# A gated mix of linear attention and feed-forward on one core: the odd feature tiles of both first token blocks placed behind the keys, roundings placed ahead of the SiLU, and another order of work into the queries

## The chip, the cores and the metric

The kernel runs on 1 core of one Trainium2 chip. The metric is the time of one execution in device microseconds. The kernel before was timed three times: the median is 782.44 us, the lowest run 778.98 us, the highest 783.22 us. One further execution was profiled.

## The reference

The input x has 2048 tokens of 640 numbers. Two branches are computed from it and mixed by a gate per token:

```python
g = sigmoid((x * gate_w).sum(-1, keepdims=True))
# branch a: linear attention, 32 heads of 20, w_phi per head
pq, pk = q @ w_phi, k @ w_phi            # per head
phi_q = concat([softmax(pq), softmax(-pq)]);  phi_k likewise
o = (phi_q @ (phi_k.T @ v)) / (phi_q @ phi_k.T.sum(tokens) + 1e-6)
a = o @ wo
# branch b: feed-forward, 1728 features
b = silu(x @ w1) @ w2
out = g * a + (1 - g) * b
```

All inputs and the output are float32.

## The kernel before, in words

Tokens lie along the free dimension for most matmuls. A float32 operand goes to TensorE (PE) as two rounded parts, a high and a low one: ScalarE (ACT) rounds the high part by a copy (L117), and VectorE (DVE) or GpSimd (POOL) subtracts it from the source for the low part (L119). Each product is then three passes: high x high, high x low, low x high (`PASSES`). The weight's low part comes last.

The work goes through five stages.

1. **Keys and values.** 16 tiles of 128 tokens (`t`). For each, `kv_proj` (L497) projects keys and values into three PSUM banks `kvp0` to `kvp2`; DVE and ACT make the two softmaxes (`k_spikes`, exp, `k_sums`), and `kv_acc` (L467) and `kv_rest` (L478) add phi_k^T v of the tile two places back into the banks `kv0` to `kv4` and into the end of `kvp2`. `kv_rest` overwrites its place in each round, so VectorE has to have added the last round to `kra` (`kv_rest_sum`, L491) before PE may go on.
2. **Behind the keys** (`t = NT - 1`, all in one hand-written order). The first feed-forward products use `kvp0` and `kvp1` while the last key tile is finished.
3. **Feed-forward, layer 1.** The tokens are 4 blocks of 512; blocks 0 and 1 are treated together, and then 2 and 3. 12 of the 13 full feature tiles go in 6 pairs. Two token blocks x two feature tiles are computed with seven products in place of eight (`product`, numbers 1 to 7, L583, 6 or 9 matmuls each), from sums and differences of the weights (`w_sums`, POOL) and of the inputs (the tiles `xt1` to `xt4`). So there are 12 pairs, `n` = 0 to 11: `h_begin` does products 1 and 2, `h_rest` products 6, 7, 4, 5, 3. Between them stand hooks (`between`), lists of small pieces of work that `plan` fills: the weights of pair n+1 are rounded in four pieces (`w_parts`, a, c, b, d), those of pair n+2 are loaded (`w_load`), and tiles of the second two blocks are loaded (`x_raw`), summed (`t_sums`, L1040) and rounded (`n_parts`, `t_parts`). The tile 12 ("l", 128 features) and the rest ("r", 64 features) are plain products (`h_std`, L537). Each result is put through SiLU on ACT and stored in DRAM (`u_out`, `r_out`).
4. **Queries.** For 16 tiles of 128 tokens: projection (L455), two softmaxes, normalisation, transposes (L1139), product with the key sums (L1223), output projection (L1256). The first four tiles (8 to 11) are done between the plain products of blocks 2 and 3; the passage to the regular rhythm (`step`) is written out by hand.
5. **Feed-forward, layer 2** (L1477), with the mix at its end.

`inorder(...)` keeps PE, DVE, ACT and POOL in the order of the program from stage 3 on, and ACT, DVE and POOL (behind the keys PE too) in stage 1 and 2. So an instruction that waits holds all that is queued behind it on its engine. SyncE (SP) issues the DMAs; its order is chosen when the program is scheduled, and a DMA that waits for its buffer holds those behind it.

Buffers that matter: `raw`, 4 buffers for loaded inputs and early results; `w`, 9 buffers for weights and their parts; 8 PSUM banks.

Two lines show how PE and the other engines are tied in a pair before the change:

```python
todo[7] += [do(w_parts, n + 1, "a"), do(w_parts, n + 1, "c")]
todo[3] += [do(w_load, n + 2)]
```

Product 7 is followed by products 4, 5 and 3, and then by product 1 of the next pair, which reads piece a.

Of the kernel before, what the change touches and what calls it, by code (L numbers as in the profile page):

```python
# [16 lines left out]
P = 128  # L17
# [41 lines left out]
def mix_kernel(ctx: ExitStack, tc: tile.TileContext, xT, wqT, wkc, wkr, wv, bd, bdc, cst, wo, w1, w1r, w2, out):  # L59
# [211 lines left out]

    def w_parts(n, k, eng="dve"):
        e, s = WR[n]
        t = W.setdefault(n, {})[k] = two(f"ws{n}{k}")
        if k == "b":
            split(t[:, 0, : 3 * P], t[:, 1, : 3 * P], e[:, D : D + 3 * P], eng)
            split(t[:, 0, 3 * P :], t[:, 1, 3 * P :], s[:, : 2 * P], eng)
        else:
            parts(t, e[:, :D] if k == "a" else s[:, 2 * P : 6 * P] if k == "c" else s[:, 6 * P : 9 * P], eng)
# [265 lines left out]

    def u_out(f, b, src, early=False):
# [4 lines left out]
    def r_out(b, src, early=False):  # L551
# [3 lines left out]
        nc.scalar.activation(o, o, AF.Silu)  # L555
        nc.sync.dma_start(u_d[NF, :FR, b * 512 : (b + 1) * 512], o)
# [35 lines left out]
    def h_begin(n, between=None, banks=None):  # L592
        between = between or {}
        s, p = divmod(n, NQ)
        done = between.get(0, [])
        for part in done:
            part()
# [9 lines left out]
        for part in between.get(1, ()):  # L607
            part()
        p2 = banks.pop(0) if banks else bank(f"p{n}_2")
        product(n, 2, p2)  # L610
        add(p2, p2, first)
        u_out(2 * p, 2 * s, p2, banks is not None)
        for part in between.get(2, ()):
            part()

    def h_rest(n, between):
        s, p = divmod(n, NQ)
# [8 lines left out]
        def after(k):  # L626
            for part in between.get(k, ()):
                part()

        p6 = mm(6)  # L630
        if second is None:
# [3 lines left out]
        p7 = mm(7)  # L635
        r = fu.tile([P, 2, 512], F32, tag="u", name=f"r{n}", bufs=3)
        add(r[:, 0, :], p7, second)
        after(7)
        p4 = mm(4)
        add(p4, p4, r[:, 0, :])  # L640
        u_out(f1, b0, p4)
        after(4)
        p5 = mm(5)
        add(r[:, 1, :], p5, second)
# [3 lines left out]
        p3 = mm(3)  # L648
        add(p3, p3, r[:, 1, :])
# [9 lines left out]
    def kv_out():  # L659

        kvm = ta.tile([P, 2, 2 * D], F32, tag="ph", name="kvm", bufs=2)[: KF + 1, 0, :]
        kvl = ta.tile([P, 2, 2 * D], F32, tag="ph", name="kvl", bufs=2)[: KF + 1, 0, :]
        for k in range(len(kvt) + 1):
            n = 2 if k < len(kvt) else 1
            lo, hi = 2 * k * KF, min((2 * k + 2) * KF, 2 * D)
            w = (hi - lo) // n
            a, b = (ap[:, lo:hi].rearrange("p (g f) -> p g f", f=w) for ap in (kvl, kvm))
# [4 lines left out]
            else:  # L672
                kv_rest_sum(NT - 1)
                nc.vector.tensor_tensor(b, kra[:, :1, RW - w :], kra[:, 1:, RW - w :], op=ALU.add)
            mask = cstt[: KF + 1, None, :w].to_broadcast([KF + 1, n, w])
            nc.gpsimd.tensor_tensor(b, b, mask, op=ALU.mult)
        kvo.extend((kvl, kvm))
# [14 lines left out]
    def n_split(b, c, t, eng="dve"):  # L692
# [12 lines left out]
        12: [lambda: w_parts(1, "a", "pool")],  # L705
# [3 lines left out]
    with inorder(ACT, DVE, POOL):  # L709
# [36 lines left out]
        with inorder(PE):  # L746
# [10 lines left out]
            n_split(0, 4, slot("xn0_4"), "pool")  # L757
# [3 lines left out]
            for k in (1, 2):  # L761
# [3 lines left out]
            b11, b21, b12 = rx[0, 0, 2], rx[0, 2, 2], rx[1, 0, 2]  # L765
            b22 = [rx[1, c] for c in (2, 3)]

            def less(o, i, j):
                nc.vector.tensor_tensor(o, i, j, op=ALU.subtract)

            less(b11, b12, b11)
            k_sums(t, eks[t])
            for k in (1, 2):
                v_part(t, k, 1)
# [804 lines left out]
```

## Time and profile before

| what | value |
|---|---|
| median of three runs | 782.44 us |
| the profiled execution | 781.32 us |
| its span, first to last instruction | 779.5 us |
| mean granted TensorE clock | 0.980 |
| PE busy | 744.7 us (96%), 4115 matmuls |
| VectorE busy | 451.9 us (58%) |
| ScalarE busy | 296.2 us (38%) |
| GpSimd busy | 331.8 us (43%) |

The span is 1.8 us shorter than the execution's own time. PE is without work in 34.8 us of the span (779.5 less 744.7). Busy is the union of the instructions, so a matmul's last part, in which the next could already have started, counts as busy.

### The profile page before, as it was taken

The page shows a single profiled execution, that of the slowest core. Times are in us where ns is not written, and L with a number is a line of the kernel's source. Part 1 is how long each engine was busy: PE and PEld are TensorE (multiplying, and loading weights), DVE is VectorE, ACT ScalarE, POOL GpSimd, SP SyncE. Part 2 cuts the span into 40 slices and gives each one's busy share as a digit, 9 for nine tenths or more (in the row PEclk, how much of TensorE's full clock was granted, in tenths as well). Part 3 has the DMA queues.
Part 4 walks back from the last instruction along what each step waited for, and adds up shares of the span by engine and source line. Part 5 has one row for each costly group of instructions (what it writes and reads, how often), then busy time and mean ns, then how long its engine had stood idle before and what let it go on. Part 6 is the DMA issues. An engine that isn't in the chain of part 4 may idle for free.

```text
span 779.5 us, 10978 instructions
## 1 busy us (share of the span) xinstructions
PE 744.7 (96%) x4115; PEld 643.4 (83%) x4115; DVE 451.9 (58%) x755; ACT 296.2 (38%) x548; POOL 331.8 (43%) x236
## 2 busy tenths in 40 slices
PE   9999999997899869999997999999998999999997
PEld 7888888885688648888986999999997888888886
DVE  5667666698647767654675776676552452232413
ACT  5344444445443354444536435433341422121110
POOL 2479888755537544133554665554300030020300
PEclk9999999999899979999998999999999999999999
DMA  9221121001443476545202111121147656172501
GB/s 317 93 69 55 34 69 34 15 0 35 145 164 114 153 226 186 184 146 172 80 0 61 55 62 56 51 69 35 35 139 236 195 166 193 48 245 76 175 26 67
DMA packets 49951, 83.41 MB, mean 107 GB/s; under 512 B 5448, under 2 KB 18904, under 8 KB 49898
## 3 DMA queue, kind: packets, MB, share of 16 engines
q1 hardware_dynamic: 49610, 82.20, 33.7%
q8 instruction: 32, 0.52, 0.3%
q10 hardware_dynamic: 288, 0.51, 0.2%
q14 instruction: 21, 0.17, 0.1%
HBM read 57.42 MB, written 25.27 MB: 106 GB/s over the span
## 4 chain that ended last, share of the span: by engine, by line
PE 56%; DMA 3%; DVE 3%; ACT 2%; issue 2%; POOL 1%; SPq 0%; DVEq 0%; ACTq 0%; POOLq 0%
PE acc L1477 24%; PE p L583 10%; PE pa L1256 9%; PE pq L455 7%; PE pn L1223 3%; PE pT L1139 2%; DMA xr<-xT 1%; PE pwq L229 1%; DMA w2rr<-w 1%; DMA wr<-w 1%; DVE eq L446 0%; DMA u_d<-u 0%; ACT eq L899 0%; PE pf L537 0%; POOL wt L270 0%
## 5 line engine op out<-in xcount | busy, mean ns | idle before, releaser
L1477 PE MATMUL acc<-u,w 128*128 128x512 f32 x780 | 179.4, 392 | 2.8 <-DVE pac L1271 2.8
L1477 PEld LDWEIGHTS acc<-u,w 128*128 128x128 f32 x780 | 147.4, 189 | 33.9 <-DVE pac L1271 3.0
L497 PE MATMUL kvp<-wh,xa 128*128 128x500 f32 (+1 forms) x420 | 92.9, 357 | 0.0
L1484 POOL TENSOR_TENSOR o<-o,y 128x512 f32<-128x512 f32 x15 | 20.2, 1381 | 152.9 <-DVE o L1483 152.9
L497 PEld LDWEIGHTS kvp<-wh,xa 128*128 128x128 f32 x420 | 71.6, 188 | 10.0
L1256 PE MATMUL pa<-oT,wo 128*128 128x256 f32 x600 | 79.6, 287 | 0.0
L119 DVE TENSOR_TENSOR u<-ur,u 128x512 fp32r<-128x512 f32 x52 | 36.1, 701 | 73.5 <-ACT u L117 73.4
L1256 PEld LDWEIGHTS pa<-oT,wo 128*128 128x128 f32 x600 | 76.1, 193 | 0.8 <-ACT oT L1232 0.8
L117 ACT CAST u<-ur 128x512 fp32r<-128x512 f32 x52 | 32.2, 623 | 107.9 <-PE acc L1477 75.1
L913 POOL TENSOR_TENSOR ez<-eq,zbc 128x1280 f32<-128x1280 f32 x16 | 47.0, 2939 | 43.2 <-ACT eq L899 43.2
L270 POOL TENSOR_TENSOR wt<-wr 128x256 f32<-128x256 f32 (+1 forms) x36 | 24.5, 681 | 83.9 <-DMA wr<-w 66.3
L548 ACT ACTIVATE u<-p 128x512 f32<-128x512 f32 x46 | 27.5, 598 | 85.0 <-issue 58.9
L119 POOL TENSOR_TENSOR ph<-ek,ph 128x1280 fp32r<-128x1280 f32 x16 | 47.4, 2963 | 28.1 <-ACT ph L117 28.1
L949 POOL TENSOR_TENSOR eq<-eq,sm 128x1280 f32<-128x1280 f32 x16 | 37.9, 2368 | 34.9 <-DVE sm L943 31.5
L497 PE MATMUL kvp<-wl,xa 128*128 128x500 f32 (+1 forms) x210 | 47.5, 356 | 0.0
L525 POOL TENSOR_TENSOR ek<-ek,st 128x1280 f32<-128x1280 f32 x16 | 37.9, 2369 | 7.7 <-ACT v L316 3.6
L497 PEld LDWEIGHTS kvp<-wl,xa 128*128 128x128 f32 x210 | 36.3, 189 | 5.4
L316 ACT CAST v<-kvp 128x360 fp32r<-128x360 f32 (+2 forms) x45 | 13.5, 336 | 69.8 <-PE kvp L497 66.5
L1483 DVE TENSOR_TENSOR o<-acc,G 128x512 f32<-128x512 f32 x20 | 13.7, 692 | 41.4 <-PE acc L1477 33.4
L455 PE MATMUL pq<-wq,xb 128*128 128x320 f32 x240 | 37.2, 312 | 0.0
L455 PE MATMUL pq<-wq,xn 128*128 128x320 f32 x240 | 36.8, 310 | 0.1
L455 PEld LDWEIGHTS pq<-wq,xn 128*128 128x128 f32 x240 | 35.6, 188 | 1.1 <-issue 0.4
(431 smaller groups left out, 1448.9 us busy)
## 6 DMA issues: line engine op xcount, KB each, us to landing
u_d<-u SPq DMA_DIRECT2D x52, 256.0 KB, 2.5
ur<-u_d SPq DMA_DIRECT2D x52, 256.0 KB, 4.2
wr<-w SPq DMA_DIRECT2D x24, 320.0 KB, 4.6
y<-fb_d SPq DMA_DIRECT2D x20, 256.0 KB, 5.9
out<-o SPq DMA_DIRECT2D x20, 256.0 KB, 4.5
w2r<-w SPq DMA_DIRECT2D x13, 320.0 KB, 3.3
fb_d<-pac SPq DMA_DIRECT2D x16, 256.0 KB, 2.1
xra<-xT SPq DMA_DIRECT2D x14, 256.0 KB, 3.3
```

Of the source, the lines that this page charges most:

```text
L117: nc.scalar.copy(hi, src)
L119: eng.tensor_tensor(lo, src, hi.bitcast(F32), op=ALU.subtract)
L270: nc.gpsimd.tensor_tensor(o[k], x, y, op=op)
L455: nc.tensor.matmul(dst, xt[c][:, hx, :], w[:, c, hw, lo : lo + n], start=first, stop=(hx == 1 and c == NC - 1))
L497: nc.tensor.matmul(kv_cols(t, lo, hi), xt[c][:, hx, :], WKV[hw][:, c, lo:hi], start=(n == 0), stop=(n == 3 * NC - 1), skip_group_check=True,)
L525: nc.gpsimd.tensor_tensor(groups(e), groups(e), spread(st[:, 1, :]), op=ALU.mult)
L548: nc.scalar.activation(o, src, AF.Silu)
L583: nc.tensor.matmul(dst, W[n][w][:, hw, j * P : (j + 1) * P], x[:, hx, :], start=(i == 0), stop=(i == len(todo) - 1))
L913: nc.gpsimd.tensor_tensor(ez, Q[t]["e"], kvb["zbc"], op=ALU.mult)
L949: nc.gpsimd.tensor_tensor(groups(q["e"]), groups(q["e"]), spread(q["sm"][:, 2 * H : 4 * H]), op=ALU.mult)
L1256: nc.tensor.matmul(pa[:, a, :], kvb["wo"][:, c, hw, ds] if c < NG else WOR[:, ds], o[:, ho, c, :] if c < NG else o[:GW, 0, c, :], start=(k ...
L1477: nc.tensor.matmul(acc[m], lhs, rhs, start=(f == OF[0] and n == 0), stop=(f == OF[-1] and n == len(todo) - 1))
```

## The change

It does four things.

1. **Roundings are cut into two halves.** `steps` gives a pair of functions, one that issues the high parts (ACT), one that issues the low parts (DVE or POOL). A hook entry that is such a pair is now issued in two places: its high part before the add that ends the product, hence ahead of that product's SiLU on ACT, and its low part behind it.
2. **Behind the keys** the plain tiles of block 1 follow those of block 0 on PE, and the last key sums (`kv_acc(15)`, `kv_rest(15)`) stand between and behind them; before, block 1's plain tiles came after pair 0, and the last key sums inside pair 1. Only pair 0 is begun in this stage (before: pairs 0 and 1). The block differences and their roundings are cut in halves of 512 and dealt out differently to DVE and POOL. The masking of the key sums comes before `w_sums(1)`. Block 1's first two chunks are no longer loaded a second time, and pair 1's piece a is no longer rounded during key tile 12.
3. **In the pairs**, piece a of pair n+1 is rounded at product 2 instead of 7, piece c at 6 instead of 7; the weights of pair n+2 are loaded after product 2 instead of 3; the tiles of blocks 2 and 3 are loaded, summed and rounded earlier and in smaller portions.
4. **Into the queries**, three instead of four transposes of the first tile pair stand before the next projection; the plain rest of block 3 stands ahead of `n_mm`; the SiLU of the last three results, with its table, moves from the passage into `step(2)`, and the two rests of blocks 2 and 3 share one tile for it; the softmax of query tile 12 comes ahead of other work on DVE and ACT.

The number of matmuls is the same (3950 matmul instructions in both programs).

The diff, cut to its core:

```diff
+    def steps(*pairs, eng="dve"):
+        def high():
+            for hi, lo, src in pairs:
+                nc.scalar.copy(hi, src)
+        def low():
+            for hi, lo, src in pairs:
+                less(lo, src, hi.bitcast(F32), eng)
+        return high, low
...
+    def hooks(between):
+        def before(k):
+            for part in between.get(k, ()):
+                if isinstance(part, tuple):
+                    part[0]()
+        def after(k):
+            for part in between.get(k, ()):
+                (part[1] if isinstance(part, tuple) else part)()
+        return before, after
...
         p2 = banks.pop(0) if banks else bank(f"p{n}_2")
         product(n, 2, p2)
+        before(2)
         add(p2, p2, first)
         u_out(2 * p, 2 * s, p2, banks is not None)
-        for part in between.get(2, ()):
-            part()
+        after(2)
...
-            less(b11, b12, b11)
             k_sums(t, eks[t])
+            n_split(0, 4, slot("xn0_4"))
...
+            for c in (2, 3):
+                n_split(1, c, room(1, c + 2, 1))
             for k in (1, 2):
                 v_part(t, k, 1)
             kv_rest_sum(t - 2)
             h_std("l", kvp[0], n1, range(NC))
             u_out(NF - 1, 0, kvp[0], True)
+            phs[t] = k_split(t, eks[t])
+            for c in range(2):
+                n_split(1, c, room(0, c + 4, 1))
+            n_split(1, 4, slot("xn1_4"))
...
             h_std("r", kvp[1], n1, range(NC))
             r_out(0, kvp[1], True)
             kv_rest(t - 1, phs[t - 1], True)
             kv_acc(t - 1, phs[t - 1])
+            kv_rest_sum(t - 1)
+            h_std("l", kvp[0], n2, (2, 3, 0, 1, 4))
+            kv_acc(t, phs[t])
+            u_out(NF - 1, 1, kvp[0], True)
+            h_std("r", kvp[1], n2, (2, 3, 0, 1, 4))
+            kv_rest(t, phs[t], True)
...
-            h_begin(0, {1: [four]}, banks)
-            two_parts()
-            h_begin(1, {1: [key_sums, lambda: parts(xt[3], b12), lambda: parts(xt[4], b21, "pool")]}, banks)
-            w_sums(1)
-            kv_out()
+            h_begin(0, {1: [t_four, lambda: kv_sums(slice(1))], 2: [*x4, lambda: kv_sums(slice(1, None))]}, [kvp[0], kvp[1]])
+            kv_mask()
+            w_sums(1)
...
         if n + 1 < 2 * NQ:
             todo[0] += [do(w_sums, n + 1)]
-            todo[7] += [do(w_parts, n + 1, "a"), do(w_parts, n + 1, "c")]
-            todo[4] += [do(w_parts, n + 1, "b")]
-            todo[5] += [do(w_parts, n + 1, "d")]
+            todo[2] += [w_steps(n + 1, "a")]
         if n + 2 < 2 * NQ:
-            todo[3] += [do(w_load, n + 2)]
+            todo[2] += [do(w_load, n + 2)]
+        if n + 1 < 2 * NQ:
+            todo[6] += [w_steps(n + 1, "c")]
+            todo[4] += [w_steps(n + 1, "b")]
+            todo[5] += [w_steps(n + 1, "d")]
...
             if n == 5:
-                todo[2] += [do(x_raw, *bc) for bc in ((2, 4), (3, 4), (3, 2), (3, 3))]
-                todo[5] += [do(n_parts, 0, 4), do(n_parts, 1, 4)]
+                todo[1] += [n_steps(0, 4)]
+                todo[7] += [n_steps(1, 4)]
+            if n == 4:
+                todo[4] += [do(x_raw, *bc) for bc in ((2, 4), (3, 4), (3, 2), (3, 3))]
...
-        t_all(0, range(4, 6))
         on(0, q_mm)
+        t_all(0, range(3, 6))
+        pf = single("pr3")
+        h_std("r", pf, n2, range(NC))
         n_all(0)
+        q_sum(11)
+        q_norm_sum(11)
+        q_parts(11)
         for gp in range(3):
             n_hi(0, gp)
-        pf = single("pr3")
-        h_std("r", pf, n2, range(NC))
-        q_sum(11)
-        more(11)
+        on(0, q_max)
+        q_inv(11)
+        q_weights(11)
+        q_mul(11)
+        r_both(3, pf, ur)
+        on(0, q_spread)
         on(1, q_mm)
-        late_out(NF, 2, ur2, FR)
-        late_out(NF - 1, 3, uf3)
-        ur3 = r_sum(3, pf)
-        late_out(NF, 3, ur3, FR)
+        on(0, q_norm)
         for gp in range(3):
             n_lo(0, gp)
+        on(1, q_max)
```

Three places show the order of the instructions, as the built programs have it. The names: `xn` and `xs` are rounded inputs of blocks 0 and 1, `rx` their raw tiles, `ek15` the exponents of the last key tile, `st15` their sums, `v0` the values, `kra` the running sum of `kv_rest`.

VectorE behind the keys, before, from the first sum of the last key tile's exponents:

```order
L523 TENSOR_REDUCE st15_1721<-ek15_1702 128x64
L524 RECIPROCAL st15_1721<-st15_1721 128x64
L318 TENSOR_TENSOR v0_110<-kvp2_80,v0_110 128x4x60
L318 TENSOR_TENSOR v0_110<-kvp2_80,v0_110 128x40
L491 TENSOR_TENSOR kra_363<-kvp2_80,kra_363 121x228
L119 TENSOR_TENSOR xs1_1730<-rx1_2_803,xs1_1730 128x512
L119 TENSOR_TENSOR xs1_1730<-rx1_3_805,xs1_1730 128x512
```

The same place in the changed kernel:

```order
L555 TENSOR_REDUCE st15_1712<-ek15_1699 128x64
L556 RECIPROCAL st15_1712<-st15_1712 128x64
L119 TENSOR_TENSOR xn0_4_1716<-rx0_4_1634,xn0_4_1716 128x512
L119 TENSOR_TENSOR xs1_1711<-rx1_2_803,xs1_1711 128x512
L119 TENSOR_TENSOR xs1_1711<-rx1_3_805,xs1_1711 128x512
L350 TENSOR_TENSOR v0_110<-kvp2_80,v0_110 128x4x60
L350 TENSOR_TENSOR v0_110<-kvp2_80,v0_110 128x40
L523 TENSOR_TENSOR kra_363<-kvp2_80,kra_363 121x228
```

Three subtractions that read two tiles of SBUF (`xn0_4`, `xs1` twice) now stand ahead of the add to `kra`; `xn0_4` was on POOL before.

ScalarE in pair 4, before, from its copy of product 1 (`q4`) to the SiLU that follows product 4 (`u0_9`); `u0_8` is the SiLU of product 2, `xn2` are tiles of block 2:

```order
L606 COPY q4_2373<-p4_1_2366 128x512
L548 ACTIVATE u0_8_2386<-p4_2_2375 128x512
L117 CAST xn2_1_2389<-xr2_1_2354 128x512
L117 CAST xn2_3_2392<-xr2_3_2358 128x512
L117 CAST ws5a_2412<-wr5_2349 128x640
L117 CAST ws5c_2415<-wt5_2360 128x512
L548 ACTIVATE u0_9_2429<-p4_4_2418 128x512
```

The same place in the changed kernel:

```order
L656 COPY q4_2385<-p4_1_2378 128x512
L279 CAST xt2_1937<-xr3_3_2220 128x512
L279 CAST ws5a_2399<-wr5_2288 128x640
L279 CAST xt3_1938<-xr3_1_2216 128x512
L584 ACTIVATE u0_8_2403<-p4_2_2389 128x512
L279 CAST ws5c_2418<-wt5_2372 128x512
L279 CAST xt4_1939<-xr2_3_2222 128x512
L279 CAST xt1_1936<-xr2_1_2218 128x512
L279 CAST ws5b_2445<-wr5_2288 128x384
L279 CAST ws5b_2445<-wt5_2372 128x256
L584 ACTIVATE u0_9_2449<-p4_4_2435 128x512
```

Piece a of pair 5 (`ws5a`) has moved ahead of the SiLU of product 2, piece b ahead of that of product 4, and the tiles `xt1` to `xt4` of the second half of the chunks have come from pair 5 into pair 4.

ScalarE on the way into the queries, before, from the last rounding of the first attention outputs (`oT0`) to the first copies of the second tile pair's transposes (`fT1`); `eq12` is the exponential of query tile 12:

```order
L1235 ACTIVATE oT0_3714<-pn0_2_3725,stk_94 120x256
L906 ACTIVATE sm11_3604<-sm11_3604,g_92 128x64
L907 ACTIVATE sm11_3604<-sm11_3604 128x32
L1170 ACT_TABLE_LOAD
L1170 ACTIVATE u2_r_3500<-u2_r_3500 64x512
L1170 ACTIVATE u3_12_3636<-u3_12_3636 128x512
L1165 COPY u3_r_3793<-pr3_3734 64x512
L1170 ACTIVATE u3_r_3793<-u3_r_3793 64x512
L847 ACTIVATE wor_h_3802<-wor_3665,stk_94 120x640
L899 ACT_TABLE_LOAD
L899 ACTIVATE eq12_3713<-eq12_3713 128x1280
L1155 COPY fT1_0_3832<-pT1_0_3817 120x512
```

The same place in the changed kernel:

```order
L1293 ACTIVATE oT0_3727<-pn0_2_3738,stk_94 120x256
L1227 COPY u23_r_3502<-pr3_3716 64x512
L963 ACTIVATE eq12_3698<-eq12_3698 128x1280
L911 ACTIVATE wor_h_3806<-wor_3661,stk_94 120x640
L1216 COPY fT1_0_3828<-pT1_0_3813 120x512
```

The two table loads and the three SiLUs are gone from this place.

More of the change, by code (lines that the diff above doesn't have):

```diff
@@ L590, in mix_kernel, with h_begin @@
     QS = {}
-    def h_begin(n, between=None, banks=None):
-        between = between or {}
+    def hooks(between):
[7 more added lines that the diff above has]
+        return before, after
+    def h_begin(n, between, banks=None):
+        before, after = hooks(between)
         s, p = divmod(n, NQ)
-        done = between.get(0, [])
-        for part in done:
-            part()
+        before(0)
+        after(0)
         p1 = banks.pop(0) if banks else bank(f"p{n}_1")
@@ L624, in mm @@
             return dst
-        def after(k):
-            for part in between.get(k, ()):
-                part()
         p6 = mm(6)
+        before(6)
         if second is None:
@@ L639, in h_rest @@
         p4 = mm(4)
+        before(4)
         add(p4, p4, r[:, 0, :])
@@ L648, in h_rest @@
         p3 = mm(3)
+        before(3)
         add(p3, p3, r[:, 1, :])
@@ L1194, in mix_kernel @@
         q_sum(10)
-        for i in range(4):
+        for i in range(3):
             t_mm(0, i, bank)
@@ L1319, in step @@
         t_all(u, range(3))
+        if u == 1:
+            on(b, lambda t: [q_sub(t, side) for side in range(2)])
+            on(a, q_sum)
         on(a, q_norm_sum, q_small, q_mul)
```

215 lines of the change are left out of this document (114 added, 101 removed).

## The prediction

> **What bounds the kernel now.** I read the page's engine rows first, then the waits of PE, then a table of PE's busy time and clock by stage, and last the timeline around each large wait.
>
> ```profile
> span 779.5 us, 10978 instructions
> PE 744.7 (96%) x4115; PEld 643.4 (83%) x4115; DVE 451.9 (58%) x755; ACT 296.2 (38%) x548; POOL 331.8 (43%) x236
> L119 DVE TENSOR_TENSOR u<-ur,u 128x512 fp32r<-128x512 f32 x52 | 36.1, 701 | 73.5 <-ACT u L117 73.4
> L117 ACT CAST u<-ur 128x512 fp32r<-128x512 f32 x52 | 32.2, 623 | 107.9 <-PE acc L1477 75.1
> ```
>
> PE is the bound, and the change leaves its matmuls as they are. So the time can fall only by what PE loses in waits and in slow clock. The other two rows give the price of one rounding of 512 columns: 0.62 us on ScalarE, 0.70 us on VectorE. PE's waits, the longest in total:
>
> ```profile
> PE p L583 <- ACT xn L117: 7.2, 1, 7.2
> PE pT L1139 <- ACT fT L1155: 5.6, 2, 4.5
> PE kvp L478 <- DVE kra L491: 3.4, 1, 3.4
> PE acc L1477 <- DVE pac L1271: 2.8, 1, 2.8
> ```
>
> Only the wait at L1477 lies in layer 2, where nothing is changed. The stages that the change touches, cut at the plain tiles behind the keys, at pair 1's product 6, at block 2's first plain tile and at the output projection, then four stretches of slow clock and one undisturbed stretch for scale:
>
> ```profile
> 172.98:216.28 43.30, 34.66 (x144) 26.54 (x142) 31.99 (x43) 20.75 (x39) 23.50 (x18) 0.92 0.30 94
> 216.28:377.61 161.33, 150.55 (x694) 124.65 (x693) 101.93 (x157) 74.50 (x147) 70.18 (x74) 0.96 0.52 164
> 377.61:435.50 57.89, 51.41 (x325) 45.46 (x323) 37.88 (x64) 25.90 (x44) 29.31 (x23) 0.94 0.12 35
> 250.00:260.00 10.00, 10.00 (x46) 8.28 (x45) 6.58 (x10) 3.38 (x7) 4.37 (x3) 1.00 0.67 220
> 192.23:199.06 6.83, 6.07 (x14) 4.79 (x15) 3.38 (x6) 5.03 (x10) 2.65 (x2) 0.50 0.22 77
> 267.32:270.73 3.41, 3.41 (x10) 2.64 (x9) 2.29 (x3) 1.30 (x3) 3.24 (x3) 0.50 0.11 42
> 289.48:294.63 5.15, 5.15 (x12) 4.08 (x13) 3.44 (x5) 2.69 (x5) 1.46 (x2) 0.50 0.90 293
> 425.72:431.16 5.44, 5.44 (x26) 5.40 (x27) 3.78 (x8) 2.15 (x5) 2.32 (x1) 0.50 0.00 0
> ```
>
> The columns are the stretch, its length, then busy time of PE, weight load, VectorE, ScalarE, GpSimd, then the clock, the DMA share and GB/s. PE is idle 8.6 us behind the keys (43.30 less 34.66), 10.8 us in the pairs, 6.5 us on the way into the queries: 25.9 us. In the slow stretches it works at half speed for 6.07 + 3.41 + 5.15 + 5.44 us, which costs half of that, 3.0 + 1.7 + 2.6 + 2.7 = 10.0 us. In the undisturbed stretch a 512-column matmul starts every 0.217 us (10.00 over 46).
>
> **Behind the keys.** Rows of before, from the timeline:
>
> ```profile
> 173.21 1.27 ACT L759 ACTIVATE ek<-ek 128x1280 f32<-128x1280 f32 x1
> 175.58 1.47 DVE L523 TENSOR_REDUCE st<-ek 128x64 f32<-128x1280 f32 x1
> 176.84 0.73 PE L537 MATMUL kvp<-xn,w_l 128*128 128x512 f32 x2 [0.74 <-POOL xn L119]
> 177.08 0.55 DVE L524 RECIPROCAL st<-st 128x64 f32<-128x64 f32 x1
> 177.41 2.47 PE L537 MATMUL kvp<-xn,w_r 128*128 128x512 f32 x10
> 177.78 2.37 POOL L525 TENSOR_TENSOR ek<-ek,st 128x1280 f32<-128x1280 f32 x1 [0.99 <-ACT xs L117]
> 177.92 0.39 DVE L491 TENSOR_TENSOR kra<-kvp,kra 121x228 f32<-121x228 f32 x1
> 178.22 3.08 DVE L119 TENSOR_TENSOR xs<-rx,xs 128x512 fp32r<-128x512 f32 x2
> 181.52 2.95 POOL L119 TENSOR_TENSOR ph<-ek,ph 128x1280 fp32r<-128x1280 f32 x1 [1.37 <-ACT ph L117]
> ```
>
> Ten matmuls take 2.47 us: nine starts 0.217 apart and a last one of 0.52. So a stop costs 0.3 us more than the gap shown, since the last matmul's tail counts as busy; with a dozen stops over 0.3 us in the three stages that is about 4 us, of which I put 2.2 here, 1.1 in the pairs, 0.8 in the passage. PE now loses here 8.6 + 2.2 + 3.0 = 13.8 us.
>
> Two subtractions of 0.70 us each took 3.08 us at 178.22: the first was held until GpSimd's 2.37 us operation ended at 180.15. The add to kra, which reads PSUM, was not held. [...]
>
> The new order step by step, with these durations. The exponential no longer waits behind a cast, so the sum starts near 173.5, the reciprocal ends near 175.5; the low part of xn0_4 follows on VectorE and ends near 176.2, when PE wants it at 175.8: 0.4 us, where 0.7 is now. GpSimd then takes the exponents (2.37 us, to about 178.3). The two low parts of xs1 come next on VectorE, are held until then and end near 179.5, and only behind them stand the value parts and the add to kra, done near 180.2. Ahead of that add they hold PE: block 0's plain tiles end near 178.7, kv_rest(14) waits 1.5 us. This is a new wait, at the head of PE's queue. Block 1's plain tiles then wait for the low parts of xs0, held by GpSimd's 2.95 us operation, and for the add of block 0's rest: 0.4 us together. Product 2 of pair 0 needs kvp1, free when ScalarE has copied block 1's rest and VectorE has added it: 0.9 us. Product 6 needs the second half of xt2's low part, two operations of GpSimd late: 1.0 us. Product 4 needs the parts of xt4, last in the queues of ScalarE and VectorE: 1.2 us. Sum: 5.4 us, where 13.8 are lost now. No wait is as long as the 3.4 us for kra now, so I expect full clock. Bounds: 4 us, if GpSimd does not come between, 9 us if each operation waits once more. The gain is 8.4 us (4.8 to 9.8).
>
> **In the pairs.** The waits there, and what made them:
>
> ```profile
> 263.28 1.19 PE L583 MATMUL p<-xn,ws5a 128*128 128x512 f32 x4 [1.13 <-ACT ws5a L117]
> 266.59 1.90 PE L583 MATMUL p<-xn,ws5a 128*128 128x512 f32 x5 [2.11 <-DVE ws5a L119]
> 280.08 0.83 SPq L1023 DMA_DIRECT2D xr<-xT  x2
> 288.80 1.26 ACT L117 CAST xn<-xr 128x512 fp32r<-128x512 f32 x2 [1.20 <-DMA xr<-xT]
> 289.48 0.79 PE L583 MATMUL p<-xn,ws6a 128*128 128x512 f32 x1 [7.22 <-ACT xn L117]
> 264.59 6.12 POOL L1040 TENSOR_TENSOR xr<-xr,xr 128x512 f32<-128x512 f32 x4
> 277.78 6.05 POOL L119 TENSOR_TENSOR xt<-xr,xt 128x512 fp32r<-128x512 f32 x4
> ```
>
> Two prices from the page, of a sum of weights and of a load of weights (320 KB, 4.6 us to landing):
>
> ```profile
> L270 POOL TENSOR_TENSOR wt<-wr 128x256 f32<-128x256 f32 (+1 forms) x36 | 24.5, 681 | 83.9 <-DMA wr<-w 66.3
> wr<-w SPq DMA_DIRECT2D x24, 320.0 KB, 4.6
> ```
>
> A pair is 54 matmuls, 11.7 us of PE. Piece a of pair 5 was rounded behind two xn tiles on ScalarE and on VectorE, beside GpSimd's input sums of 264.59, and PE waited 1.1 and 2.1 us. It now stands at product 2, 39 matmuls or 8.4 us ahead of its use in place of 27 or 5.9 us, and no xn tile is ahead of it in that pair. The 7.2 us came from a tile of block 2 whose load was issued at 280.08, when pair 5 was nearly over, and landed at 288.8. Its load now follows product 4 of pair 4, its rounding product 1 of pair 5; even if the load waits for GpSimd's last splits of pair 4, it has 10 us or more. Both waits go, and with them two slow stretches: 10.8 + 1.1 + 4.3 = 16.2 us. What is late next: GpSimd, which no longer waits for weights, has five sums of weights (5 x 0.68 = 3.4 us; so far it stood idle for 66.3 us in all for their loads) and either 6.1 us of input sums or 6.0 us of low parts in each of pairs 1 to 4: about 9.5 of 11.7 us. It fits, so I leave 0.5 us, bounds 0 and 5. SyncE's new order, loads of blocks ahead of loads of weights, is covered by the same slack. More than the waits can't be gained, as PE's work is the same. The gain is 15.7 us (11.2 to 16.2).
>
> [...] Rows: PE ran at half clock from 267.32 on, behind an idle time of 2.11 us, and from 289.48 behind 7.22. [...]
>
> **Into the queries.** Rows:
>
> ```profile
> 413.58 4.56 PE L455 MATMUL pq<-wq,xn 128*128 128x320 f32 x30
> 415.04 2.37 POOL L949 TENSOR_TENSOR eq<-eq,sm 128x1280 f32<-128x1280 f32 x1
> 418.04 1.60 DVE L1240 TENSOR_TENSOR oT<-pn,oT 128x512 fp32r<-128x512 f32 x3
> 419.52 1.28 ACT L899 ACT_TABLE_LOAD   x1
> 423.79 1.27 ACT L899 ACTIVATE eq<-eq 128x1280 f32<-128x1280 f32 x1 [2.98 <-DVE eq L446]
> 425.72 0.68 PE L1139 MATMUL pT<-ident,eq 128*120 128x128 f32 x2 [4.47 <-ACT fT L1155]
> ```
>
> Lost now: 6.5 + 0.8 + 2.7 = 10.0 us. The 4.47 us: the copies of the transposes stood behind the exponential on ScalarE, that behind VectorE's softmax, that behind oT. Now the exponential can end near 418, so the copies follow the transposes. Gone too is the other wait of pT on fT, 5.6 less 4.5 = 1.1 us, since only three transposes now stand ahead of the projection. What is late next is GpSimd's weighting of tile 11, which ends at 417.41 as before, while PE, 2 us earlier, wants it at 416.3: 1.1 us. Then three transposes wait for copies and banks, 0.3 us each, and the next tile's weighting comes 0.4 us late: 2.4 us in all, bounds 1.4 and 5. The table load and the two SiLUs that move into step 2 (1.28 + 2 x 0.6 = 2.5 us) lie beside a projection of 4.56 us and cost nothing; without that cover they would hold the next copies, and PE, by 2.5 us. Gain 7.6 us (5 to 8.6).
>
> **The sum.** 8.4 + 15.7 + 7.6 = 31.7 us, bounds 21 and 34.6. The profiled execution's 781.32 us (span 779.5 and 1.8 around it) becomes 749.6; it was 1.1 us under the median 782.44, so I say 750.
>
> **The rivals.**
> *GpSimd's lock stretches the pairs.* With GpSimd no longer waiting for weights, each of VectorE's low parts can be held by it, as at 178.22, by up to 2.4 us, and the pieces come late pair after pair. [...] Against it, pair 5 has neither sums nor splits of inputs, and a piece has 8 us to spare. If it decides, pairs 2 to 5 each lose a stop of 2 us and a slow stretch of 1.7 us: 4 x 3.7 = 15 us, 765 us. [...]
> *The waits only change place.* Behind the keys and in the passage the new waits (kra, xt2, xt4, tile 11) cost as much as the old, and the lock takes 12 us of the pairs' gain: 31.7 - 8.4 - 7.6 - 12 = 3.7 us, 778 us. Against: the old waits are longer than any of the new chains.
> *SyncE's queue (slower).* Loads of weights now stand behind block loads that wait for GpSimd to free their buffers. Landing (4.6 us), 3.4 us of sums and 1.3 us of rounding make 9 us from issue to use. An issue later than about 11 us after product 2 decides, for then every pair is longer by what is more. Late by 8 us in each of pairs 2 to 6, it takes back all and more: 750 + 40 = 790 us. Against: GpSimd's 9.5 us per pair fits, so the lag doesn't build up.
>
> **How the numbers follow.** A measurement of this kernel tells 0.5%, 4 us, from no change. Chances: forecast 0.70, lock in the pairs 0.19, only displaced 0.05 (over half of it within 0.5%), SyncE's queue 0.06. The range takes in the bounds of the sum (747 to 761), three microseconds below for the spread of runs (778.98 to 783.22), and most of the second case: 743 to 765. Faster 0.90, same 0.04, slower 0.06.
>
> **What would show it.** In the changed kernel's profile, PE's waits on xn and ws5a are gone from the pairs and the clock is 1.00 in them; kv_rest(14) waits for kra about 1.5 us; the wait of the transposes on fT is under 1 us; the stretch from the plain tiles to pair 1's product 6, whose work is the same, takes about 35 us in place of 43.3. It is wrong if PE waits for weights' low parts or for loads of wr in pairs 2 to 6, or if half clock appears behind the keys.

## The result, and the profile after

The changed kernel takes 752.48 us (median of 4 runs, 751.80 to 753.64) against 780.71 us for the kernel before, run beside it (median of 4, 778.80 to 783.22): ratio 0.9638, 95% interval 0.9601 to 0.9675. The profiled execution took 753.64 us, its span is 751.9 us. The forecast was 750, with a range of 743 to 765.

From the page of the changed kernel:

```profile
PE 736.4 (98%) x4115; PEld 637.4 (85%) x4115; DVE 452.7 (60%) x759; ACT 296.3 (39%) x550; POOL 329.8 (44%) x236
```

PE's waits, the longest in total (columns as before):

```profile
PE p L621 <- ACT xn L279: 5.4, 1, 5.4
PE kvp L510 <- DVE kra L523: 1.2, 1, 1.2
...
PE pT L1200 <- POOL eq L1013: 1.0, 2, 0.7
PE kvp L621 <- DVE u_r L590: 0.6, 1, 0.6
```

The old waits of 2 us and more are gone but for the one on kra, which is down from 3.4 to 1.2 us. There is one new long one, of 5.4 us, on a rounded input tile. The stages, cut where PE begins the same work as in the three stages shown of before, then all that follows, then the half-clock stretch:

```profile
173.23:207.26 34.03, 31.74 (x145) 24.36 (x143) 29.98 (x41) 19.19 (x39) 21.68 (x19) 1.00 0.28 85
207.26:361.25 153.99, 148.56 (x693) 123.68 (x692) 104.59 (x164) 76.87 (x151) 71.35 (x74) 0.98 0.55 176
361.25:411.20 49.95, 48.71 (x325) 42.98 (x323) 38.46 (x64) 24.17 (x45) 26.82 (x21) 1.00 0.11 35
411.20:751.90 340.70, 335.20 (x2004) 294.72 (x2004) 163.04 (x247) 100.44 (x173) 93.75 (x50) 1.00 0.35 111
280.85:286.92 6.07, 6.07 (x14) 4.26 (x15) 5.78 (x11) 2.78 (x6) 2.84 (x4) 0.50 0.55 174
```

Against the stages of before: behind the keys 43.30 - 34.03 = 9.3 us gained, in the pairs 161.33 - 153.99 = 7.3, on the way into the queries 57.89 - 49.95 = 7.9, and behind it 344.0 (779.5 - 435.5) - 340.7 = 3.3. The first stage begins 0.25 us later than before; the sum is 27.6 us, the difference of the spans. So two terms of the forecast came out (8.4 and 7.6), one came out at less than half (15.7), and one that stood at nothing gave 3.3.

**The pairs.** The chain of waits through pair 6 (start, length, what):

```profile
271.18 7.91 DMA u_d<-u
...
279.17 0.60 ACT u L584
...
280.28 0.53 ACT xn L279
...
280.85 7.38 PE p L621 x18
```

Read it from below. PE waits for a rounding of `xn3_2` on ScalarE. That stands behind a SiLU, and the SiLU writes one of the two buffers for results (`ur`), whose last store took 7.91 us. What SyncE issued around that store, in the timeline:

```profile
269.60 0.39 SPq L1046 DMA_DIRECT2D consts<-bd  x1
...
270.50 0.36 SPq L1049 DMA_DIRECT2D consts<-kv_d  x1
271.18 0.34 SPq L585 DMA_DIRECT2D u_d<-u  x1
```

The sizes of these transfers, by the DMA issues from 268 to 274 us:

```profile
consts<-kv_d SPq DMA_DIRECT2D x1, 605.0 KB
consts<-bd SPq DMA_DIRECT2D x1, 360.0 KB
consts<-cst SPq DMA_DIRECT2D x1, 96.0 KB
```

1061 KB of constants went out just ahead of a store of 256 KB. The list of the change says that the tiles of blocks 2 and 3 are rounded earlier. In the full diff, `xn3_2` and `xn3_3` move the other way: before, they were rounded behind product 1 of pair 6, now at product 7. (`xn3_0` and `xn3_1` move back too, by one product of pair 7, and PE doesn't wait for them.) Their first user is product 3; only products 4 and 5, 18 matmuls, lie between:

```diff
             if p == 0:
-                todo[1] += [do(n_parts, 1, 2), do(n_parts, 1, 3)]
+                todo[7] += [n_steps(1, 2), n_steps(1, 3)]
```

**Layer 2.** Its start, in the timeline of before:

```profile
586.69 0.41 DVE L1271 COPY pac<-pa 128x256 f32<-128x256 f32 x1
587.15 3.36 PE L1477 MATMUL acc<-u,w 128*128 128x512 f32 x9 [2.85 <-DVE pac L1271]
```

And of after:

```profile
560.38 2.25 PE L1549 MATMUL acc<-u,w 128*128 128x512 f32 x9
...
562.97 2.34 PE L1549 MATMUL acc<-u,w 128*128 128x512 f32 x9 [0.34 <-DVE pac L1329]
```

An accumulator still waits for the copy of the queries' last output, but it is no longer the first one: PE does nine matmuls ahead of it. In the built programs, that last output (`pa7_4`) lies in PSUM bank 0 before and in bank 5 after; the accumulators take banks 0, 7, 6, 5, 4 in both. The passage now takes its banks in another sequence, and that shifts the rotation down to here.

### The profile page after: what moved, and what is told of

It is laid out like the page before. It is cut to its first block, busy times and chain, and to the rows that moved or that the text cites. A ratio compares the mean times of both kernels' runs of the same rounds, so it can differ in the third digit from the quotient of the medians.

```text
span 751.9 us, 10994 instructions
## 1 busy us (share of the span) xinstructions
PE 736.4 (98%) x4115; PEld 637.4 (85%) x4115; DVE 452.7 (60%) x759; ACT 296.3 (39%) x550; POOL 329.8 (44%) x236
## 4 chain that ended last, share of the span: by engine, by line
PE 85%; DVE 8%; ACT 2%; POOL 2%; DMA 2%; issue 1%; SPq 0%; DVEq 0%; POOLq 0%; ACTq 0%
PE acc L1549 24%; PE p L621 18%; PE kvp L529 15%; PE pa L1314 8%; PE pq L487 7%; PE kv L499 2%; PE pn L1281 2%; PE pT L1200 2%; PE kvp L388 1%; PE kvq L388 1%; DMA u_d<-u 1%; PE pwk L377 1%; DVE eq L478 1%; PE pwq L229 1%; POOL ez L977 1%
## 5 line engine op out<-in xcount | busy, mean ns | idle before, releaser
L1314 PE MATMUL pa<-oT,wo 128*128 128x256 f32 x600 | 77.8, 283 | 0.1
L1314 PEld LDWEIGHTS pa<-oT,wo 128*128 128x128 f32 x600 | 74.2, 188 | 1.1 <-ACT oT L1290 0.8
L270 POOL TENSOR_TENSOR wt<-wr 128x256 f32<-128x256 f32 (+1 forms) x36 | 26.6, 739 | 53.8 <-DVE ws7b L273 11.2
L487 PEld LDWEIGHTS pq<-wq,xb 128*128 128x128 f32 x240 | 35.2, 188 | 1.5 <-issue 1.2
```

The source lines that it names most:

```text
L270: nc.gpsimd.tensor_tensor(o[k], x, y, op=op)
L487: nc.tensor.matmul(dst, xt[c][:, hx, :], w[:, c, hw, lo : lo + n], start=first, stop=(hx == 1 and c == NC - 1))
L1314: nc.tensor.matmul(pa[:, a, :], kvb["wo"][:, c, hw, ds] if c < NG else WOR[:, ds], o[:, ho, c, :] if c < NG else o[:GW, 0, c, :], start=(k ...
```

## The experiments

Theory after the profile: (1) the pairs lost 8.7 us (5.4, a tail of 0.3, 3.0 for half clock) because two roundings stand in ScalarE's queue behind a SiLU that waits for a store; (2) the store is late because of the constants; (3) layer 2 gained by the banks; (4) what the change took out of the pairs came from the places of the roundings, as forecast. Each had its rival.

**xn3 early.** The two roundings back where they were before the change:

```diff
-                todo[7] += [n_steps(1, 2), n_steps(1, 3)]
+                todo[1] += [n_steps(1, 2), n_steps(1, 3)]
```

> The changed kernel, with the roundings of the last two chunks of block 3 (xn3_2, xn3_3) issued behind product 1 of pair 6 in place of product 7, so ahead of the SiLU of product 2 on ScalarE. Theory (ScalarE's queue): PE's 5.43 us wait in pair 6 comes from these two roundings standing behind a SiLU that waited 4.59 us for its buffer; the SiLU still waits, but PE no longer does: the 5.43 us, a tail of 0.3 and the half-clock stretch behind it (3.0 us) go, 752.5 - 8.7 = 743.8 us. Rival (changed place): what is queued behind the SiLU, piece c of pair 7 above all, is then awaited instead and PE stops for 3 to 5 us at pair 7's product 6: 749 to 752 us.

745.60 us (743.81 to 747.10, 4 runs), ratio to before 0.9544, interval 0.9519 to 0.9569. PE's waits from 200 to 345 us, whole:

```profile
PE p L621 <- ACT u L584: 0.5, 1, 0.5
```

ScalarE around the place, in the timeline:

```profile
275.14 1.15 ACT L279 CAST xn<-xr 128x512 fp32r<-128x512 f32 x2
...
280.62 0.60 ACT L584 ACTIVATE u<-p 128x512 f32<-128x512 f32 x1 [3.69 <-DMA u_d<-u]
```

The SiLU still waits, 3.69 us, now behind the roundings, and PE does not wait. 6.9 us of the expected 8.7 show in the medians, with runs that spread over 3.3 us. The profiles leave this spread out: from pair 1's product 6 to block 2's first plain tile the stretch takes 146.01 us in place of 153.99, 8.0 us less, and the profiled run came to the stage behind the keys 1.4 us later than that of the changed kernel. Theory 1 holds; one wait of 0.5 us is all that is listed in the pairs.

**Constants apart.** The loads of `cst` and `kv` written two pairs later in the program:

```diff
+            if p == 2:
+                todo[5] += [load_b_rest]
```

> The changed kernel, with two of the three loads of constants (cst 96 KB, kv 605 KB) issued two pairs later; the third (360 KB) and the order of all roundings stay. Theory (the store is held by the loads): the store issued at 271.2 us lay behind 1061 KB of constants and so held its buffer for 8 us; with 360 KB ahead of it, the SiLU's wait of 4.59 us falls to 1.7 us or less (as at the two SiLUs before it), PE's 5.43 us wait falls under 2 us and the half clock behind it goes: 743.8 to 746 us. Rival (the loads of weights hold the store, or the order of the SyncE queue): the SiLU's wait stays over 4 us and the time stays at 752.5 us.

753.31 us (752.21 to 753.54), ratio 0.9641, interval 0.9618 to 0.9663. The run tells nothing on the theory, since the loads did not move. SyncE's order is chosen when the program is scheduled, and they went out where they were:

```profile
269.37 0.37 SPq L1051 DMA_DIRECT2D consts<-kv_d  x1
270.06 0.33 SPq L585 DMA_DIRECT2D u_d<-u  x1
```

**Constants held.** The same with something to wait for:

```diff
     def load_b_rest():
+        for t in (kvb["cst"], kvb["kvm"]):
+            nc.vector.memset(t[:1, :1], 0.0)
```

> The changed kernel; the loads of cst and kv (701 KB of 1061) now write tiles in which VectorE sets one element during pair 8, so SyncE cannot issue them in pair 6. Theory (the store is held by the loads): the store issued near 271 us has 360 KB of constants ahead of it in place of 1061; at the 200 to 250 GB/s of that stretch it lands about 3 us sooner, the SiLU's wait of 4.59 us falls to 2 us or less, PE's wait of 5.43 us falls under 2.5 us: 746 to 748 us. Rival (loads of weights or the store itself set the 8 us): SiLU and PE wait as before, 752.5 us.

747.49 us (746.85 to 748.53), ratio 0.9566, interval 0.9531 to 0.9602. ScalarE at the same SiLU, in the timeline:

```profile
274.68 0.60 ACT L584 ACTIVATE u<-p 128x512 f32<-128x512 f32 x1 [0.96 <-DMA u_d<-u]
```

PE's longest wait in the pairs:

```profile
PE p L621 <- ACT xn L279: 1.0, 1, 1.0
```

The SiLU's wait fell from 4.59 to 0.96 us, PE's from 5.43 to 0.97, and half clock is gone from the pairs. From the issue of the store whose buffer this SiLU takes to the SiLU itself are 3.7 us (270.95 to 274.68), where the changed kernel has 8.0 (271.18 to 279.17). Theory 2 holds: with 701 KB of constants less ahead of the store, this time is 4.3 us shorter. How the transfers share the queue was not shown.

**Passage undone.** The passage into the queries as it was before the change (all of part 4 of the change put back):

```diff
+        t_all(0, range(4, 6))
         on(0, q_mm)
-        t_all(0, range(3, 6))
-        pf = single("pr3")
...
+        on(0, q_logits)
+        on(0, q_norm, q_sum)
```

> The changed kernel, with the passage into the queries put back as it was before the change. Theory (additive stages, and banks): the passage loses its 7.6 us again, and with it the wait at the first accumulators of layer 2 returns (2.85 us, a tail of 0.3 and a half-clock stretch of 3.4 us that costs 1.7; between the two profiles this place shows 4.0 us), because the number of PSUM banks handed out in the passage decides which bank the first accumulator gets: 752.5 + 7.6 + 4.0 = 764.1 us. Rival (layer 2 gained from something else, such as the times of loads): the wait in layer 2 stays at 0.3 us: 760.1 us.

763.28 us (762.15 to 764.02), ratio 0.9770, interval 0.9746 to 0.9793, 10.8 us more than the changed kernel. PE's waits:

```profile
PE pT L1200 <- ACT fT L1216: 5.6, 2, 4.5
PE acc L1538 <- DVE pac L1332: 2.1, 1, 2.1
```

Both waits are back together, and in the built program `pa7_4` is in bank 0 again, so the gain in layer 2 belongs to the passage. By the same cuts as above, the passage takes 56.93 us in this profile, 7.0 more than the 49.95 of the changed kernel, where 7.6 were forecast. All that follows takes 2.8 us more, and the pairs 0.6, with a wait on `xn` of 6.4 us in place of 5.4.

**Banks in the kernel before.** Three one-element memsets take the next three banks ahead of layer 2:

```diff
+            if b == 0:
+                for s in range(3):
+                    nc.vector.memset(ps.tile([P, 512], F32, tag="acc", name=f"skip{s}", bufs=8)[:1, :1], 0.0)
             acc = [ps.tile([P, 512], F32, tag="acc", name=f"acc{b}_{m}", bufs=8) for m in range(NC)]
```

> The kernel before the change, with three one-element memsets on VectorE that take the next three PSUM banks just ahead of layer 2, so that its first accumulator no longer gets the bank that the last output of the queries still holds. Theory (banks): the wait of 2.85 us at the start of layer 2, its tail of 0.3 and its half clock (1.7 us) go: 4.0 to 4.9 us faster than before the change, ratio 0.994 to 0.995. Rival (PE waits there for the rounded inputs or weights of layer 2, whose loads were late): the wait stays, at another releaser, ratio 1.000.

777.41 us (775.07 to 781.57, 12 runs), ratio 0.9955, interval 0.9937 to 0.9974. The start of layer 2:

```profile
585.38 4.94 PE L1477 MATMUL acc<-u,w 128*128 128x512 f32 x21
585.58 0.42 DVE L1271 COPY pac<-pa 128x256 f32<-128x256 f32 x1
```

PE runs through 21 matmuls from before the last copy on. In the built program the accumulators now take banks 5, 4, 3, 1 and 2. The loads of layer 2 stand where they did, so theory 3 holds; it is worth 3.2 us here (780.60, the median of the 17 runs of before that go with it, less 777.41), where 4.0 to 4.9 were expected. In the profiles, the two stretches from the output projection to layer 2 and through layer 2 take 4.7 us less; the pairs, which this edit does not touch, took 2.0 us more in the profiled run.

**Pieces late.** On top of xn3 early, pieces a and c and the loads of weights at their old places:

```diff
-            todo[2] += [w_steps(n + 1, "a")]
+            todo[7] += [w_steps(n + 1, "a"), w_steps(n + 1, "c")]
...
-            todo[2] += [do(w_load, n + 2)]
+            todo[3] += [do(w_load, n + 2)]
```

> The kernel with xn3 early (745.6 us), with pieces a and c of the next pair's weights rounded behind product 7 again, and the loads of weights behind product 3. Theory of the prediction (the place of piece a made the two waits on ws5a, 1.1 and 2.1 us): the waits come back where input tiles are rounded beside it, in one or two pairs: 3.2 us, tails 0.6 and a half clock of 1.7, so 749 to 754 us. Rival (the waits came from the input tiles ahead of piece a and the late loads, which stay mended here): no wait comes back, 745.6 us.

754.16 us (753.71 to 757.21), ratio 0.9660, interval 0.9616 to 0.9704: 8.6 us more than xn3 early. PE's two longest waits in the pairs:

```profile
PE p L621 <- ACT ws7a L279: 1.9, 1, 1.9
PE p L621 <- ACT ws6a L279: 1.9, 1, 1.9
```

Waits on piece a come back, in four pairs (the other two are 0.5 and 0.2 us, on `ws3a` and `ws4a`), where one or two were expected, and behind the longer two a half-clock stretch each of 3.4 us, which cost 1.7 each: 4.5 + 3.4 and four tails of 0.3 are 9.1 us. The stretch of the pairs is 9.0 us longer than with xn3 early. The loads moved too, but they are not what PE waited for: GpSimd sums the weights of pairs 6 and 7 from 265.86 and 277.45 on, and ScalarE rounds their piece a at 268.50 and 284.58 only, right behind a SiLU that waited itself. The one ahead of `ws7a`:

```profile
284.08 0.60 ACT L584 ACTIVATE u<-p 128x512 f32<-128x512 f32 x1 [3.14 <-DMA u_d<-u]
```

Theory 4 holds for the place of piece a. The late load of block 2's tile was not put back; that the 7.2 us went with it is read from the two profiles alone.

**Behind the SiLU.** On top of xn3 early, high and low parts together behind the SiLU:

```diff
-                if isinstance(part, tuple):
-                    part[0]()
...
-                (part[1] if isinstance(part, tuple) else part)()
+                for step in part if isinstance(part, tuple) else (part,):
+                    step()
```

> The kernel with xn3 early (745.6 us), with every high part of a cut pair issued behind the SiLU again, together with its low part. Theory of the prediction (a piece has about 8 us to spare, so 1 to 2 us later on ScalarE cost nothing): 745 to 747 us. Rival (being ahead of the SiLU is what takes the waits out of the pairs, since a SiLU can wait up to 4 us for its buffer's store): PE stops for 1 to 4 us at pieces or input tiles in several pairs, 750 to 760 us.

765.52 us (765.17 to 765.63), ratio 0.9795, interval 0.9759 to 0.9831: 19.9 us more than xn3 early, against an expectation of nothing. Two of eleven waits of PE from 200 to 345 us:

```profile
PE p L621 <- ACT xn L279: 3.2, 1, 3.2
...
PE p L621 <- ACT ws3a L279: 2.3, 1, 2.3
```

The theory's "8 us to spare" falls. Nor is it the rival's reason: ScalarE waited for a store once there, for 2.9 us in all. What follows is drawn from the order and not shown by a run of its own: with both parts behind the SiLU, each product needs VectorE's add, ScalarE's SiLU, ScalarE's high part, VectorE's low part, and only then the next add, one after the other.

**No sums.** The kernel of the last run, behind the SiLU, without GpSimd's eight sums of input tiles; it leaves them out of the computation:

```diff
-                todo[4] += [do(t_sums, i)]
```

> The kernel of the run behind the SiLU (765.5 us), without GpSimd's eight sums of the input tiles of blocks 2 and 3 in pairs 1 and 3 (about 12 us of GpSimd); these sums are left out of the computation, their tiles are still loaded and rounded. Theory (the shared lock stretches VectorE's low parts, and behind the SiLU each stretched low part holds the next add, the next SiLU and the next rounding): PE's stops in pairs 1 to 5, 11 of the 18 us, shrink by 4 us or more: under 761.5 us. Rival (the round trip ScalarE, VectorE, ScalarE alone makes them, whatever GpSimd does): 764 to 766 us.

760.97 us (759.92 to 761.50), ratio 0.9742, interval 0.9714 to 0.9771: 4.5 us less. PE's waits in the pairs, the longest, and the one behind the first sums:

```profile
PE p L621 <- ACT ws6a L279: 2.2, 1, 2.2
...
PE p L621 <- ACT ws3a L279: 0.5, 1, 0.5
```

The wait behind the first sums (piece a of pair 3) falls from 2.3 to 0.5 us, and VectorE's two low parts of pair 2's piece b, which ran beside these sums for 1.22 and 1.50 us, take 0.69 and 0.68: GpSimd's hold, the lock of the expectation, is part of it. In the profiles the pairs take 157.97 us in place of 164.47, 6.5 us less; the medians show less because this run has a half-clock stretch behind the keys, at 199.16, ahead of all the sums that were taken out. But 12.0 of the 18.5 us that the pairs lose against xn3 early stay, and one wait got longer (on `ws6a`, 0.8 to 2.2 us). How much of those the other work of GpSimd makes (sums of weights, low parts), and how much the round trip alone, stays open.

**Kra first.** On top of xn3 early, the add to `kra` ahead of the low parts of `xs1`:

```diff
             for k in (1, 2):
                 v_part(t, k, 1)
             kv_rest_sum(t - 2)
+            for low in lows:
+                low()
```

> The kernel with xn3 early (745.6 us), with the two low parts of xs1 on VectorE behind the value parts and the add to kra in place of ahead of them. Theory (the two subtractions, held by GpSimd, made kv_rest(14) wait 1.16 us): the wait goes and nothing else is late, 744.2 us. Rival (the same hold only moves on): block 1's plain tiles or pair 0 wait for xs1 by as much, 745.6 us or more.

744.48 us (743.99 to 745.18, 6 runs), ratio 0.9527, interval 0.9498 to 0.9555, not to be told from xn3 early. PE's longest wait there:

```profile
PE kvp L569 <- DVE xs L119: 1.2, 1, 1.2
```

The wait on `kra` is gone, and one on `xs`, as long, stands there instead: the rival. The hold is the same in both orders (VectorE's last two low parts of `xs` take 3.62 us in each, beside a GpSimd operation of 2.94 us with xn3 early and 2.95 here), and PE meets it either way.

**All mended.** Xn3 early, constants held, kra first, and in block 1's tile 12 the passes with an input's low part last:

```diff
+        if last:
+            todo.sort(key=lambda k: k[2])
```

> The changed kernel with xn3 early, with the loads of cst and kv held to pair 8, with kra first, and with the passes that read an input's low part last in block 1's plain tile 12. Theory: to the 745.6 us of xn3 early, the wait of 1.2 us that moved from kra to xs goes with a tail of 0.3, as its matmuls now come 10 starts (2.2 us) into the tile, and the stop of 0.46 us on ScalarE's late SiLU in pair 8 goes with 0.3: 743.3 us, ratio 0.951 to 0.953. Rival (the holds only change place once more): 745 to 746 us.

744.75 us (744.13 to 745.14), ratio 0.9536, interval 0.9514 to 0.9559. PE's waits from 172 to 345 us, whole:

```profile
PE kvp L623 <- DVE u_r L592: 0.6, 1, 0.6
PE p L623 <- DVE xs L273: 0.3, 1, 0.3
```

The long waits are gone, and the time is that of the run before, not 743.3. The timeline of block 1's tile 12 says why:

```profile
180.19 3.63 DVE L119 TENSOR_TENSOR xs<-rx,xs 128x512 fp32r<-128x512 f32 x2 [0.70 <-ACT xs L117]
...
183.75 0.68 DVE L119 TENSOR_TENSOR xn<-rx,xn 128x512 fp32r<-128x512 f32 x1
184.49 0.50 PE L571 MATMUL kvp<-xn,w_l 128*128 128x512 f32 x1
```

The tile's last matmul needs its last low part, which VectorE has at 184.43 in this order too, behind two low parts that took 3.63 us beside GpSimd's operation of 2.96 us (from 179.72 on). PE counts as idle for less of the stage (1.5 us in place of 2.3), but the stage is as long as in the run before, 34.04 against 34.06 us: PE meets the hold in small steps. The rival, then. The three kernels with xn3 early and no other loss (744.5 to 745.6 us) beat both given kernels; among them there is no difference that these runs can tell.

## Why the prediction was right, and where it was wrong

**Right: PE is the bound, and the gain is what PE no longer loses.** PE's busy time, in which the half clock and the tails count, fell by 8.3 us, its time without work by 19.3 (34.8 to 15.5): together the 27.6 us.

**Right: behind the keys.** 34.0 us instead of the 35 forecast, at full clock. The hold on VectorE came as worked out, with the add to kra behind it:

```profile
175.99 2.62 POOL L557 TENSOR_TENSOR ek<-ek,st 128x1280 f32<-128x1280 f32 x1 [1.17 <-ACT xs L117]
176.31 3.45 DVE L119 TENSOR_TENSOR xs<-rx,xs 128x512 fp32r<-128x512 f32 x2
176.44 0.30 PEld L569 LDWEIGHTS kvp<-xn,w_l 128*128 128x128 f32 x2 [0.51 <-DVE xn L119]
...
180.63 0.34 PE L510 MATMUL kvp<-ph,v 128*121 128x228 f32 x1 [1.16 <-DVE kra L523]
...
197.75 1.10 PE L621 MATMUL p<-xs,ws0b 128*128 128x512 f32 x2 [0.33 <-DVE xs L273]
```

The two subtractions took 3.45 us, the wait for kra was 1.16 us (1.5 forecast), that for kvp1 0.6 (0.9). The last row is product 4, which reads xt4: its first two matmuls with low parts start 0.72 and 0.60 us behind the one before, and the next one 0.34, where 0.23 is usual, so xt4 cost about 1.0 us (1.2 forecast). In the same way xn0_4 held PE for 0.4 us (0.4 forecast), a stop too short for the list of waits, and xt2 for 0.3 (1.0). Block 1's plain tile 12 waited for nothing that can be seen (0.4).

**Right: into the queries.** 7.9 us against 7.6; the waits left are those on tile 11's weighting (0.68 us, 1.1 forecast) and one of 0.39 us ahead of the projection that ends the stage. The three of 0.3 us that were forecast on copies and banks are in no list.

**Wrong: the pairs, 7.3 us instead of 15.7.** The waits on ws5a and on the late tile of block 2 went, as the prediction said; its signs of failure (weights' low parts, loads of wr) did not show. But two of its signs of success did not show either: PE waited 5.4 us on an xn tile, and the clock of the pairs was 0.98. The step that failed is "Both waits go, and with them two slow stretches", with 0.5 us left for what is late next, bounds 0 and 5; it cost 8.7. It followed one input tile, whose rounding moves earlier, and took that for all of them; two others move from product 1 to product 7 of pair 6, which the prediction does not mention. And the search for what is late next asked for GpSimd and SyncE only. ScalarE's queue was counted in roundings, without the SiLU's own wait for its buffer, though the trace of before had rows on it. ScalarE's waits for stores with such a SiLU from 200 to 345 us, before:

```profile
ACT u L548 <- DMA u_d<-u: 3.4, 2, 2.2
```

And after:

```profile
ACT u L584 <- DMA u_d<-u: 14.4, 7, 4.6
```

Why there are more of them was not shown. That a faster PE brings the results closer together, so that two buffers of 256 KB no longer cover a store, fits the run behind the SiLU (2.9 us of such waits), but not pieces late, which has 20.6 us of them although its PE is no faster than in the changed kernel. No run has a third buffer, which would tell.

**Wrong: "Only the wait at L1477 lies in layer 2, where nothing is changed".** The wait of 2.8 us was read as untouched because no line of layer 2 changes. It hung on which PSUM bank comes last, and that is set by every allocation ahead of it. This error of 3.3 us and the one in the pairs (8.4) had opposite signs; with 0.9 and 0.3 us more than forecast in the two other stages, and 0.25 less for the later start, the profiled gain is 27.6 us where 31.7 were forecast. That the median came out 2.5 us from the forecast is therefore luck in part: without the 3.3 us that nothing in the prediction foresaw, it would be about 755.8 us.

**The rival of the lock** did not decide: the hold lengthens VectorE's low parts in the pairs (one of 256 columns took 1.51 us at 219.40, beside GpSimd's sums of 6.00 us from 216.06 on, where 0.42 is taken at 268.85), but PE waited for no piece of the weights there. What the prediction calls a lock is in the runs only this, that VectorE's low parts take longer beside GpSimd's operations. No run shows the rival's term, a stop of 2 us with a slow stretch of 1.7 us in each of four pairs, or the 12 us that the second rival has the lock take: the changed kernel lost 5.4 us and one slow stretch in the pairs, at a rounding behind a SiLU. The run behind the SiLU shows that the 8 us which a piece has by PE's order do not keep it so, as the prediction had it: there the pieces have the same 8 us, and the time is 765.5 us. That it is because a piece no longer stands between two adds fits the order, and was not shown apart from the rest.

## What to carry to other kernels

Where an engine keeps the program's order, look at what each instruction ahead of the moved one can itself wait for, stores of its output buffer included, and look for steps that a large reordering moves later. A wait at a place that the change does not touch can hang on the rotation of buffers, so compare the banks or slots of both built programs before calling it unchanged. And a DMA is moved by its dependences, not by its line, where the scheduler sets the queue's order: the load of `kv` stayed in pair 6, at 269.37 us, when its line moved two pairs on, and left it only with something to wait for.

## What the runs showed of the hardware

The first rival of the prediction has a slow stretch follow each stop of 2 us. It is not the length of a wait alone that decides: the clock halved behind a wait of 1.9 us and was full through both stretches around one of 3.2. Two stretches of 3.41 us of the run pieces late, around a wait of 1.9 us (PE's busy time is the first number behind the length, the clock stands third from the end):

```profile
266.26:269.67 3.41, 1.52 (x7) 0.94 (x7) 2.94 (x5) 1.99 (x5) 3.33 (x5) 1.00 0.51 175
269.67:273.08 3.41, 3.41 (x10) 2.63 (x9) 3.41 (x7) 2.12 (x6) 0.03 (x1) 0.50 0.28 93
```

Two of the run behind the SiLU, around its wait of 3.2 us:

```profile
286.69:290.10 3.41, 1.69 (x8) 1.07 (x6) 1.17 (x2) 0.47 (x2) 0.00 (x0) 1.00 0.51 173
290.10:293.51 3.41, 1.94 (x7) 1.22 (x8) 1.90 (x3) 1.92 (x4) 0.00 (x0) 1.00 0.31 94
```

In the profile of before, the clock is 0.50 from 192.23 to 199.06, 267.32 to 270.73, 284.39 to 294.63, 424.34 to 431.16 and 588.18 to 591.59 us: stretches of 2, 1, 3, 2 and 1 times 3.413 us, with 20, 4, 38 and 46 times that between them. Laid on the grid of such steps that each run's own half-clock stretches show, the clock halved behind a stretch in which PE was busy for 1.52 of 3.41 us, and in the other run stayed full behind one with 1.69, although that wait was the longer one: it lay across two stretches (in that run a half-clock stretch began at 262.80, seven steps of 3.413 us ahead of 286.69).

No sharp limit follows. On the grid of the run no sums, whose half-clock stretch behind the keys began at 199.16, this stretch lies right ahead of it:

```profile
195.75:199.16 3.41, 1.83 (x7) 0.98 (x6) 2.19 (x5) 2.21 (x6) 0.69 (x1) 1.00 0.33 124
```

PE was busy for 1.83 us in it, more than the 1.69 us behind which the clock stayed full. What exactly is counted stays open.
